# More warming products for TensorE in the run-in, and one set of weights listed two tiles later, in a kernel of dynamic convolution and maxout

## The chip, the cores and the metric

The kernel runs on one core of one Trainium2 chip. The metric is the device time of one execution in microseconds, the median of several runs. Times inside the execution are read from one profiled execution of the same kernel and count from the start of its span. PE is TensorE, DVE is VectorE, ACT is ScalarE, POOL is GpSimd and SP is SyncE, whose queue issues most DMAs.

## What is computed

Inputs are `x` (8 x 4160 x 192), `weight_gen` (8 x 4160 x 8 heads x 7 taps) and three matrices of an expert layer. Cut to what matters:

```python
w = exp(weight_gen - max) / (sum over the 7 taps + 1e-9)      # a softmax per token and head
out[b, s, h, :] = sum over k of w[b, s, h, k] * x_pad[b, s + k, h, :]   # causal, 24 elements a head
x = out.reshape(33280, 192)
h1 = x @ w1          # 192 -> 1024
h2 = x @ w2
g = maximum(h1, h2)
return g @ w_out     # 1024 -> 192
```

The kernel uses max(h1, h2) = h1 + relu(h2 - h1). It forms the difference of the two weight matrices once (`wd`) and the product `w1 @ w_out` once (`w10`), so that a result is relu(x wd) w_out + x w10.

## The kernel before

The 33280 tokens are 260 columns of 128 tokens. Columns are worked in batches of 16: batch 0 is columns 0 to 15, batch 2 columns 32 to 47. One tile is one 128x1024 block of hidden values, as much work as one column, so there are 260 tiles. They go in groups: eight of two tiles (0 to 15), then groups of three.

The work of the engines is this. ScalarE makes the weights (exponential, logarithm, exponential), applies the ReLU to the hidden values and copies results out of PSUM. VectorE multiplies `x` by the weights for all seven taps (`mul`), adds the taps (`adds`), and does the sums (`red`) and shifts (`shift`) of the softmax. TensorE does the hidden and the output products. From column 32 on, the sums are transposed by a DMA (`transpose`); for the first 32 columns TensorE sums and transposes in one step, with an identity as the moving operand:

```python
def sum_transpose(u, taps=range(K)):
    ...
    yps = ps[...].tile([P, 1024], FP32, name="yps", tag="op")
    for k in range(6):
        for t in taps:
            for r in range(2):
                nc.tensor.matmul(yps[...], lhsT=m_t[half(r), at:at + P], rhs=ident[half(r), half(r)], ...)
    yt = pyt.tile(...)
    nc.scalar.copy(out=..., in_=...)          # the cast of yps to yt
```

The softmax weights of a part of a batch are an exponential on ScalarE of what `shift` left:

```python
def shift(b, i=0, of=1):
    nc.vector.tensor_tensor(out=w_t, in0=w_t, in1=..., op=ALU.subtract)   # minus the logarithm of the sum

def weights(b, o):
    ...
    nc.scalar.activation(out=..., in_=_sub(wg_ts[b], ...), func=AF.Exp)
```

A group is listed by `hidden`. `relay` is a no-op on ScalarE that waits for the first output products, and the second ones wait for it:

```python
def hidden(g, now=(), between=lambda: None, beside=lambda: None, ahead=lambda: None):
    t0, n = GROUPS[g]
    rd = room(g)
    for t in range(t0, t0 + n - 1):
        hid_tile(t)
    if now:
        out_room(now, ...)
        last = out_first(now)
    ...
        for t in range(t0, t0 + n - 1):
            relu(rd, t, 1)
    if now:
        go = relay(last)
    hid_tile(t0 + n - 1)
    ...
    relu(rd, t0 + n - 1, 1)
    ahead()
    if now:
        out_second(now, go)
        evac(now[0] // 2, len(now) // 2)      # copies results out of PSUM, on ScalarE
    ...
```

The run-in, cut. `warm` is a PSUM tile that nothing reads:

```python
def keep_warm(times):
    for _ in range(times):
        nc.tensor.matmul(warm[:, 0:512], lhsT=ident, rhs=_sub(ident, 0, [[0, 4], [1, P]]),
                         start=True, stop=True, skip_group_check=True)

keep_warm(20)
w_diff(0, nc.scalar.copy)
sum_transpose(0)
keep_warm(2)
mul(0, 4)
nc.scalar.copy(out=w1["E"][:, HF:F], in_=ws["E", 0][:, HF:F])
hidden(0)
nc.scalar.copy(out=w1["T"], in_=ws["T", 0])
w_diff(1, nc.vector.tensor_copy)
mul(0, 8)
sum_transpose(1)
exp_sum(1)
red(1)
adds(0, 8, True)
hidden(1)
ln(1)
shift(1)
mul(0, 12)
...
def end_of_1():
    shift(2)
    adds(1, 8, True)
    mul(1, 12)
    exp_sum(3)
    red(3)
    adds(1, 12, True)

early = {
    3: (none, rest_of_1),
    4: (lambda: sum_transpose(4, LEFT), lambda: (end_of_1(), weights(2, 0))),
    5: (lambda: sum_transpose(5, LEFT), none),
    ...
}
```

In the steady stage a list says at which tile each logarithm, exponential and set of weights is put into ScalarE's queue; the logarithm of a batch (`ln`) is listed a few tiles later for later batches.

Of the kernel before, what the change touches and what calls it, by code (L numbers as in the profile page):

```python
# [17 lines left out]
def _sub(base: bass.AP, off: int, dims):  # L18
    ap = [list(base.ap[0])] + [[int(s), int(c)] for s, c in dims]
    return dataclasses.replace(base, offset=base.offset + off, ap=ap)  # L20
# [3 lines left out]
def kernel(  # L24
# [28 lines left out]
    def pieces(b):  # L53
        n = BATCHES[b][1]
        at, done = [], 0
        for w in (4, 4, 4, 4) if b < 2 else (8, 8) if n == 16 else (n,):
            at.append((done, w))
            done += w
        return at
# [81 lines left out]
    def ln(b):  # L141
        nc.scalar.activation(out=s_ts[b], in_=s_ts[b], func=AF.Ln)  # L142
# [7 lines left out]
    def weights(b, o):  # L150

        w = dict(pieces(b))[o]
        if b not in en_ts:
            en_ts[b] = pen.tile([P, 16 * WGC * 2], BF16, name="en_t", tag="en")
        J = 2 if w == 4 and b < 2 else 1
        N = w * H // J
        for j in range(J):
            nc.scalar.activation(  # L158
                out=_sub(en_ts[b], (o * WGC + j * N * K) * 2, [[2 * N, K], [2, N], [1, 2]]),
                in_=_sub(wg_ts[b], (o * H + j * N) * K, [[1, K], [K, N], [0, 2]]), func=AF.Exp,  # L160
            )
# [62 lines left out]
    def half(j):  # L224
        return slice(64 * j, 64 * j + 64)


    LEFT = (0, 1, 2, K - 1)

    def sum_transpose(u, taps=range(K)):  # L230

        b, o, n = UNITS[u]
        assert n == 4
        yps = ps["r" if "r" in ps else "o"].tile([P, 1024], FP32, name="yps", tag="op")
# [3 lines that stand above are left out]
                    at = (K * o + t * n) * D + k * P  # L238
                    nc.tensor.matmul(  # L239
                        yps[:, r * 512 + k * 64:r * 512 + (k + 1) * 64],  # L240
                        lhsT=m_t[half(r), at:at + P], rhs=ident[half(r), half(r)],
                        start=(k == 0 and t == taps[0]), stop=(t == taps[-1]),
                        skip_group_check=True,
                    )
        yt = pyt.tile([P, 8 // 2 * 3 * P], BF16, name="yt", tag="yt")
        nc.scalar.copy(out=_sub(yt, 0, [[64, 2], [P, 6], [1, 64]]),  # L246
                       in_=_sub(yps, 0, [[512, 2], [64, 6], [1, 64]]))
        yt_ts[u] = yt
# [18 lines left out]
    def hid_tile(t):  # L267


        u = TILES[t][0]  # L270
        fs, w = chunks(t)
        for f in fs:
            for s in range(3):
                for j in range(2):
                    nc.tensor.matmul(  # L275
                        hid_out(t, f, j), lhsT=wd[half(j), s * F + f * P:s * F + (f + 1) * P],
                        rhs=_sub(yt_ts[u][half(j), :], (s + j) % 3 * P, [[3 * P, w // P], [1, P]]),
                        start=(f == fs[0] and s == 0), stop=(f == fs[-1] and s == 2),
                        skip_group_check=True,
                    )  # L280

    def relu(rd, t0, n):

        (hd, at), k = hd_at[t0], rd_at[t0][1]
        nc.scalar.activation(out=rd[:, k * 1024:(k + n) * 1024], in_=hd[:, at:at + n * 1024],  # L285
                             func=AF.Relu)
# [34 lines left out]
    def out_first(now):  # L321

        for c in now[::2]:
            u, i, _ = column(c)
            for s in range(3):
                for j in range(2):
                    nc.tensor.matmul(  # L327
                        op_out(c + j),
                        lhsT=yt_ts[u][half(j), (3 * i + (s + j) % 3) * P:(3 * i + (s + j) % 3 + 1) * P],
                        rhs=w10[half(j), s * D:(s + 1) * D], start=(c == now[0] and s == 0),  # L330
                        stop=False, skip_group_check=True,
                    )
            for f in range(FCH):
                last = [out_hidden(c + j, f, j) for j in range(2)]
        return last

    def out_second(now, go):

        for c in now[::2]:
            for f in range(FCH):  # L340
                for j in range(2):
                    mm = out_hidden(c + 1 - j, f, j)
                    if c == now[0] and f == 0:
                        tc.add_manual_dep(mm.ins, go.ins.name, SYNC, reason="bank of the other half")

    def relay(last):

        go = nc.scalar.nop()  # L348
        for mm in last:
            tc.add_manual_dep(go.ins, mm.ins.name, SYNC, reason="bank of the other half")  # L350
        return go
# [50 lines left out]
    OUTS, c = [[], [], []], 0  # L402
# [8 lines left out]
    def room(g):  # L411

        t0, n = GROUPS[g]
        if "c" in ps:
            ab = ps["ab"].tile([P, 2048], FP32, name="hd2", tag="ab")
            for t in range(t0, t0 + n - 1):
                hd_at[t] = ab, (t - t0) * 1024
            hd_at[t0 + n - 1] = ps["c"].tile([P, 1024], FP32, name="hd1", tag="c"), 0
        else:
            for t in range(t0, t0 + n):  # L420
                hd_at[t] = ps["h"].tile([P, 1024], FP32, name="hdp", tag="hd"), 0
        rd = prd.tile([P, 3 * 1024], BF16, name="rd_t", tag="rd")
        for t in range(t0, t0 + n):
            rd_at[t] = (rd, t - t0)
        return rd

    def out_room(now, tag=None):
        tag = tag or ("r" if "r" in ps else "o")
        w, name = {"ab": (2048, "ab"), "c": (1024, "c")}.get(tag, (1024, "op"))
        tile_ = ps[tag].tile([P, w], FP32, name="op_ps", tag=name)  # L430
        for c in now:
            op_at[c // 2] = tile_, (c - now[0]) // 2 * D
# [9 lines that stand above are left out]
            out_room(now, "ab" if n == 1 and "ab" in ps else None)  # L442
            last = out_first(now)
        if len(now) > 2:
            relu(rd, t0, n - 1)
        else:
# [5 lines that stand above are left out]
        if len(now) > 2:  # L452
            beside()
# [4 lines that stand above are left out]
            evac(now[0] // 2, len(now) // 2)  # L458
        between()
        if len(now) <= 2:  # L460
            beside()
# [25 lines left out]
    with tc.tile_pool(name="pstage", bufs=1) as pstage:  # L487
# [101 lines left out]
        def keep_warm(times):  # L589

            for _ in range(times):
                nc.tensor.matmul(warm[:, 0:512], lhsT=ident, rhs=_sub(ident, 0, [[0, 4], [1, P]]),
                                 start=True, stop=True, skip_group_check=True)

        keep_warm(20)
        w_diff(0, nc.scalar.copy)
        sum_transpose(0)
        keep_warm(2)
        mul(0, 4)


# [67 lines left out]
# [9 lines that stand above are left out]
    none = lambda: None  # L678
    early = {
        3: (none, rest_of_1),  # L680
        4: (lambda: sum_transpose(4, LEFT), lambda: (end_of_1(), weights(2, 0))),
        5: (lambda: sum_transpose(5, LEFT), none),
        6: (lambda: (weights(2, 8), ln(3), sum_transpose(6, LEFT)), lambda: load_x(3, 0, 8)),
        7: (lambda: sum_transpose(7, LEFT), none),
    }
# [48 lines left out]
    def steps(g, tiles):  # L734

        if tiles:
            softmax_steps(g)
        for t in tiles:
            extra(t)
# [6 lines left out]
    for g in range(4, len(GROUPS)):  # L746
        if GROUPS[g][1] == 3 and "c" not in ps:
            later_ps()
        tiles = [t for t in range(GROUPS[g][0], sum(GROUPS[g])) if t >= 16]
        if g in early:  # L750
            hidden(g, OUTS[g], early[g][0], ahead=lambda: (weights(1, 12), ln(2)) if g == 4 else None)
            early[g][1]()
            steps(g, tiles)
        else:
            hidden(g, OUTS[g], beside=lambda: steps(g, tiles))
# [30 lines left out]
```

The softmax here doesn't subtract the row's maximum and nothing guards it: scores larger than these inputs give would overflow.

## Time and profile before

| | before |
|---|---|
| time, median of 3 runs | 416.42 us (416.41 to 416.79) |
| span of the profiled execution | 415.6 us |
| TensorE busy | 396.6 us, 95% |
| VectorE busy | 377.2 us, 91% |
| ScalarE busy | 359.4 us, 86% |
| GpSimd busy | 73.2 us, 18% |

A line of the time line reads: start in us, duration in us (of a run of alike instructions as one), engine, line of the kernel, operation, result <- operands, shape, count; in square brackets the idle time of that engine just before it and what ended it. A line of a stretch reads: stretch and its length, then busy time and instructions of PE, PEld (weight loads), DVE, ACT and POOL, then the granted TensorE clock, the share of the DMA engines and GB/s. A line of a DMA queue reads: packets, MB, and the time of the packets as a share.

### The profile page before, as it was taken

How to read it: one execution, taken by the hardware profiler on the slowest of the kernel's cores; microseconds unless marked ns; L12 is line 12 of the kernel's file. 1: busy time of each engine (PE TensorE's matmuls, PEld its weight loads, DVE VectorE, ACT ScalarE, POOL GpSimd, SP SyncE). 2: the span in 40 equal slices, each digit the busy share in tenths (PEclk: the TensorE clock that was granted, in tenths of full speed). 3: DMA queues.
4: the chain of work that ended last, by engine and by line, in shares of the span. 5: the costliest groups of instructions: out<-in, count | busy, mean ns of one | idle time of the engine just before them, and what ended most of it. 6: DMA issues, size and time to landing. Idle time of an engine off the chain costs nothing.

```text
span 415.6 us, 15816 instructions
## 1 busy us (share of the span) xinstructions
PE 396.6 (95%) x7262; PEld 316.6 (76%) x7262; DVE 377.2 (91%) x218; ACT 359.4 (86%) x425; POOL 73.2 (18%) x102
## 2 busy tenths in 40 slices
PE   5788899999999999999999999999999999999994
PEld 2678899777777787777877778777787777777793
DVE  5999999999999999999999999999999999998000
ACT  5798989998989998899998999989999988888761
POOL 1510101222210222221002121220122220210000
PEclk9699999999999999999999999999999999999998
DMA  8966427766656966866786498478658658635423
GB/s 235 255 170 175 108 74 166 158 166 146 171 119 124 248 154 120 232 165 103 189 203 161 93 254 184 75 241 171 131 101 245 162 103 207 150 77 191 98 79 115
DMA packets 60243, 65.68 MB, mean 158 GB/s; under 512 B 47602, under 2 KB 48498, under 8 KB 60177
## 3 DMA queue, kind: packets, MB, share of 16 engines
q1 hardware_dynamic: 51904, 40.47, 35.6%
q0 software_dynamic: 8128, 24.11, 28.3%
q8 instruction: 57, 0.93, 0.9%
q10 hardware_dynamic: 144, 0.10, 0.1%
q14 instruction: 10, 0.07, 0.1%
HBM read 35.96 MB, written 25.56 MB: 148 GB/s over the span
## 4 chain that ended last, share of the span: by engine, by line
PE 59%; DVE 21%; ACT 12%; issue 3%; DMA 3%; SPq 1%; DVEq 0%; ACTq 0%
PE op_ps L315 27%; PE hd L275 26%; DVE m_t L173 11%; ACT rd_t L285 7%; PE op_ps L327 5%; DVE m_t L189 4%; DVE m_t L195 3%; DMA ws1T<-in_moe_w_dram 2%; ACT en_t L158 1%; DMA yt<-y_t 1%; DVE wg_t L147 1%; DVE y_t L198 1%; PE hdp L275 1%; ACT o_t L371 1%; DVE sum_t L139 1%
## 5 line engine op out<-in xcount | busy, mean ns | idle before, releaser
L285 ACT ACTIVATE rd_t<-hd 128x1024 bf16<-128x1024 f32 (+1 forms) x206 | 234.6, 1188 | 28.3 <-PE hd L275 26.9
L315 PE MATMUL op_ps<-wo,rd_t 64*128 64x192 bf16 x4160 | 211.0, 243 | 1.0 <-ACTq L348 0.9
L315 PEld LDWEIGHTS <-rd_t 64*128 64x128 bf16 x4160 | 181.2, 94 | 16.8 <-ACTq L348 1.5
L275 PE MATMUL hd<-yt,wd 64*128 64x512 bf16 (+1 forms) x1584 | 187.8, 360 | 1.7 <-ACT rd_t L285 1.1
L173 DVE TENSOR_TENSOR m_t<-xb_t,en_t 128x10752 bf16<-128x10752 bf16 (+1 forms) x37 | 187.5, 5070 | 0.3 <-ACT en_t L158 0.3
L275 PEld LDWEIGHTS <-wd 64*128 64x128 bf16 x1776 | 95.4, 95 | 45.6 <-issue 5.7
L215 POOL CAST gate<-yt 128x1 f32<-128x1 bf16 x29 | 37.3, 1287 | 276.9 <-DMA yt<-y_t 276.9
L189 DVE TENSOR_TENSOR m_t<-m_t 128x4608 bf16<-128x4608 bf16 (+1 forms) x34 | 79.5, 2338 | 0.1
L371 ACT COPY o_t<-op_ps 128x384 f32<-128x384 f32 (+1 forms) x99 | 57.1, 589 | 13.4 <-PE op_ps L315 13.2
L327 PE MATMUL op_ps<-w,yt 64*128 64x192 bf16 x780 | 55.9, 243 | 1.8 <-ACT o_t L371 0.9
L327 PEld LDWEIGHTS <-yt 64*128 64x128 bf16 x780 | 38.6, 94 | 18.8 <-issue 3.5
L195 DVE TENSOR_TENSOR m_t<-m_t 128x3072 bf16<-128x3072 bf16 (+1 forms) x29 | 49.9, 1722 | 0.1
L158 ACT ACTIVATE en_t<-wg_t 128x896 bf16<-128x896 f32 (+2 forms) x45 | 35.2, 818 | 1.1 <-DVE wg_t L147 1.1
L198 DVE TENSOR_TENSOR y_t<-m_t 128x1536 bf16<-128x1536 bf16 (+1 forms) x29 | 27.3, 941 | 0.5
L361 DVE COPY o_t<-op_ps 128x192 f32<-128x192 f32 x1 | 0.4, 357 | 26.5 <-ACT o_t L361 26.5
L139 DVE TENSOR_REDUCE sum_t<-e_t 128x64 f32<-128x448 f32 (+2 forms) x30 | 19.5, 650 | 3.5 <-ACT e_t L127 3.5
L147 DVE TENSOR_TENSOR wg_t<-wg_t,sum_t 128x280 f32<-128x280 f32 (+4 forms) x45 | 22.0, 489 | 0.6 <-ACT sum_t L142 0.4
L115 POOL DMA_DIRECT2D xb_t<-in_x_dram x32 | 17.3, 539 | 24.2 <-DVE m_t L173 15.6
L127 ACT ACTIVATE e_t<-wg_t 128x896 f32<-128x896 f32 (+1 forms) x17 | 16.0, 940 | 2.8 <-DMA wg_t<-in_weight_gen_dram 2.8
L285 ACT ACTIVATE rd_t<-hdp 128x1024 bf16<-128x1024 f32 x16 | 16.1, 1033 | 1.9 <-PE hdp L275 1.9
L275 PE MATMUL hdp<-yt,wd 64*128 64x256 bf16 x192 | 14.0, 287 | 1.9 <-ACT yt L246 0.9
L239 PE MATMUL yps<-ident,m_t 64*128 64x64 bf16 x492 | 9.6, 198 | 2.9 <-DVE m_t L173 2.9
(46 smaller groups left out, 73.1 us busy)
## 6 DMA issues: line engine op xcount, KB each, us to landing
out_dram<-o_t SPq DMA_DIRECT2D x28, 768.0 KB, 4.3
xb_t<-in_x_dram POOLq DMA_DIRECT2D x28, 384.0 KB, 5.1
wg_t<-in_weight_gen_dram POOLq DMA_DIRECT2D x14, 448.0 KB, 5.9
xb_t<-xb_t POOLq DMA_DIRECT2D x16, 288.0 KB, 5.3
out_dram<-o_t SPq DMA_DIRECT2D x8, 384.0 KB, 2.7
wg_t<-in_weight_gen_dram SPq DMA_DIRECT2D x2, 448.0 KB, 4.9
xs<-in_x_dram SPq DMA_DIRECT2D x2, 384.0 KB, 6.7
xb_t<-in_x_dram POOLq DMA_DIRECT2D x1, 768.0 KB, 6.8
```

The costliest lines, as they stand in the source:

```text
L147: nc.vector.tensor_tensor(out=w_t, in0=w_t, in1=_sub(s_ts[b], hs.start, [[1, hs.stop - hs.start], [0, K]]), op=ALU.subtract)
L158: nc.scalar.activation(out=_sub(en_ts[b], (o * WGC + j * N * K) * 2, [[2 * N, K], [2, N], [1, 2]]), in_=_sub(wg_ts[b], (o * H + j * N) * K ...
L173: nc.vector.tensor_tensor(out=m_out, in0=x_in, in1=_sub(en_ts[b], o * WGC * 2, [[2, K * n * H], [0, G // 2], [1, 2]]), op=ALU.mult,)
L189: nc.vector.tensor_tensor(out=taps(0, 1, 3), in0=taps(0, 1, 3), in1=taps(3, 1, 3), op=ALU.add)
L195: nc.vector.tensor_tensor(out=taps(0, 2, 2), in0=taps(0, 2, 2), in1=taps(1, 5, 2), op=ALU.add)
L198: nc.vector.tensor_tensor(out=_sub(y_ts[b], o * D, [[64, 2], [P, 3 * w // 2], [1, 64]]), in0=taps(0, 1, 1), in1=taps(2, 1, 1), op=ALU.add,)
L215: nc.gpsimd.tensor_copy(out=gate, in_=yt[:, 0:1])
L275: nc.tensor.matmul(hid_out(t, f, j), lhsT=wd[half(j), s * F + f * P:s * F + (f + 1) * P], rhs=_sub(yt_ts[u][half(j), :], (s + j) % 3 * P, ...
L285: nc.scalar.activation(out=rd[:, k * 1024:(k + n) * 1024], in_=hd[:, at:at + n * 1024], func=AF.Relu)
L315: return nc.tensor.matmul(op_out(c), lhsT=rd[half(r), k * 1024 + at:k * 1024 + at + P], rhs=wo[half(r), f * D:(f + 1) * D], start=False, s ...
L327: nc.tensor.matmul(op_out(c + j), lhsT=yt_ts[u][half(j), (3 * i + (s + j) % 3) * P:(3 * i + (s + j) % 3 + 1) * P], rhs=w10[half(j), s * D: ...
L371: nc.scalar.copy(out=_sub(o, c % 24 * D, [[D, len(qs)], [h * D, 2], [1, D]]), in_=_sub(tile_, at + (qs[0] - p) * D, [[D, len(qs)], [512, 2 ...
```

## The change

Three edits. The warming products ahead of the first sums become 30 instead of 20, and those behind them 6 instead of 2: they are there to keep TensorE's clock up while it waits for VectorE's first product and for the first cast. And `weights(2, 0)`, the weights of columns 32 to 39, is no longer listed at the end of group 4 (tiles 8 and 9). It is listed in group 5 (tiles 10 and 11), behind the two ReLUs of that group and ahead of its copy of results, so that ScalarE comes to it later.

```diff
-        keep_warm(20)
+        keep_warm(30)
         w_diff(0, nc.scalar.copy)
         sum_transpose(0)
-        keep_warm(2)
+        keep_warm(6)
         mul(0, 4)
@@
-        4: (lambda: sum_transpose(4, LEFT), lambda: (end_of_1(), weights(2, 0))),
+        4: (lambda: sum_transpose(4, LEFT), end_of_1),
@@
-            hidden(g, OUTS[g], early[g][0], ahead=lambda: (weights(1, 12), ln(2)) if g == 4 else None)
+            hidden(g, OUTS[g], early[g][0], ahead=lambda: {4: lambda: (weights(1, 12), ln(2)), 5: lambda: weights(2, 0)}.get(g, none)())
```

## The prediction

> **What bounds the kernel now.** I read the page's totals first, then the chain that ended last, then the idle times of VectorE, TensorE and ScalarE, because three engines are nearly full and a total cannot say which of them sets the end.
>
> ```profile
> PE 396.6 (95%) x7262; PEld 316.6 (76%) x7262; DVE 377.2 (91%) x218; ACT 359.4 (86%) x425; POOL 73.2 (18%) x102
> PE 59%; DVE 21%; ACT 12%; issue 3%; DMA 3%; SPq 1%; DVEq 0%; ACTq 0%
> ```
>
> VectorE's 91% is an average: table 2 of the page has it at 9 tenths until slice 36 and then almost nothing. Until 345 us it is practically never idle. The chain in order of time lies on TensorE from 52 to 260 us, on VectorE from 261 to 344 us, then passes through one transposing DMA to TensorE. The crossing in the time line:
>
> ```profile
> 344.12 5.75 DVE L173 TENSOR_TENSOR m_t<-xb_t,en_t 128x10752 bf16<-128x10752 bf16 x1
> 344.35 1.27 SPq L207 DMA_TRANSPOSE yt<-y_t  x1
> 349.56 0.82 PE L275 MATMUL hd<-yt,wd 64*128 64x512 bf16 x6 [0.60 <-DMA yt<-y_t]
> ```
>
> The transposing DMA is issued 0.15 us after VectorE's last add, and TensorE stands still 0.60 us until it lands. It is TensorE's only wait of any size after 300 us; afterwards TensorE works through to the end. So the end is the later of two runners at this point: VectorE plus one DMA, and TensorE, which is only 0.60 us behind in need. A gain has to reach **both** to reach the end.
>
> The early stage shows where either can gain. The granted clock of one stretch, TensorE's early groups, and VectorE's first wait in the run-in:
>
> ```profile
> 13.35:20.20 6.85, 5.91 (x122) 4.56 (x116) 6.71 (x7) 5.51 (x7) 2.59 (x5) 0.50 1.25 223
> ```
> ```profile
> 12.12 1.43 PE L239 MATMUL yps<-ident,m_t 64*128 64x64 bf16 x84 [2.90 <-DVE m_t L173]
> 13.48 1.03 PE L592 MATMUL warm<-ident 128*128 128x512 bf16 x2
> 15.46 2.74 PE L275 MATMUL hdp<-yt,wd 64*128 64x256 bf16 x24 [0.94 <-ACT yt L246]
> 17.97 2.41 PE L239 MATMUL yps<-ident,m_t 64*128 64x64 bf16 x84
> ```
> ```profile
> 20.42 0.80 ACT L246 CAST yt<-yps 128x768 bf16<-128x768 f32 x1 [0.23 <-PE yps L239]
> 21.11 0.95 ACT L127 ACTIVATE e_t<-wg_t 128x896 f32<-128x896 f32 x1
> 22.10 1.09 DVE L139 TENSOR_REDUCE sum_t<-e_t 128x128 f32<-128x896 f32 x1 [0.72 <-ACT e_t L127]
> ```
>
> The clock is half for 6.85 us: PEclk, the third number from the end, is 0.50. The same 84 small products take 1.43 us at full clock and 2.41 at half; ScalarE's cast waits for them, its exponential stands behind the cast, and VectorE waits 0.72 us for that exponential. The second place:
>
> ```profile
> 40.50 1.09 DVE L147 TENSOR_TENSOR wg_t<-wg_t,sum_t 128x896 f32<-128x896 f32 x1
> 41.62 1.04 ACT L158 ACTIVATE en_t<-wg_t 128x896 bf16<-128x896 f32 x1 [1.05 <-DVE wg_t L147]
> 41.70 0.61 PEld L315 LDWEIGHTS <-rd_t 64*128 64x128 bf16 x16 [1.17 <-ACTq L348]
> ```
>
> ScalarE stands 1.05 us at the weights of columns 32 to 39 because VectorE has just begun their shift, and TensorE stands behind ScalarE's no-op.
>
> **What the Trainium skill says.** "TensorE: Matmul & The Clock Gate", Part 1 (The HAM clock gate): the array runs at half clock until a free-running window of about 3.4 us has been busy, and returns to half after an idle one. The trace agrees: the warming products start 0.43 us apart, 0.21 us after 6.40 us; the clock falls at about 13.36 us and returns at about 20.19, 6.83 us or two windows. Counted back on that grid, the window from 9.95 to 13.36 held 1.2 us of work and lost the clock. The window from 6.54 to 9.95 held some 2.6 us and kept it. "PSUM — Partial Sum Buffer", Engine vs sequencer instructions: ScalarE's queue is strictly first in, first out, and a no-op runs on its sequencer. The trace agrees: the no-op passes 0.08 us after the blocked exponential starts, before the ReLU listed ahead of it begins at 42.56. "DMA: Bandwidth & Descriptors", Queues, rings and completion order: each DMA engine takes its queues in turn, a packet at a time. I use it below for why one transpose is slow; the trace shows the coincidence, not the cause.
>
> **Part 1, the warming products.** Ten more at 0.21 us take 2.1 us: they end at 9.22 + 2.1 = 11.3 us, inside the 2.90 us in which TensorE waited for VectorE's product, so they delay nothing. The window to 13.36 then holds about 1.4 + 1.2 = 2.6 us of work and should keep the clock. Six products behind the first sums then take 6 x 0.21 = 1.3 us and end near 14.8, ahead of 15.46, when the cast ends for which the hidden products wait. Those 24 take 1.48 us (as the same group does later at full clock) and not 2.74; the next 84 start at 16.9 (VectorE's product is done at 16.13) and end near 18.4 instead of 20.4. On ScalarE: ReLU from 16.3 to 18.25 (two, 1.0 each), the cast of w1 to 19.2, the cast of the sums to 19.9, the exponential from 19.8 to 20.75. Before, it started at 21.11, so ScalarE gains 1.3 us. VectorE is free at 18.42 + 2.96 = 21.4; its 0.72 us wait vanishes. What follows on VectorE needs ScalarE results that are also 1.3 us earlier, so I count **0.72 us for VectorE, 1.3 us for ScalarE and TensorE**. Nothing is taken away: 14 products and 14 loads are added, all into idle time.
>
> **Part 2, the weights two tiles on.** The 1.04 us activation is moved, not removed. Its old place made ScalarE wait for VectorE's shift, which ends at 41.6 - 0.7 = 40.9 after part 1. ScalarE would be there at 40.56 - 1.3 = 39.3. In the new place two ReLUs come first (39.3 to 41.2), so the shift is done, the weights end near 42.1, and the copy of results starts near 42.0 instead of 44.37: TensorE and ScalarE are now **2.3 us** ahead (1.3 from part 1, about 1.0 from the wait). VectorE needs these weights only at 47.90 - 0.7 = 47.2, so it gains and loses nothing here.
>
> **Two small waits further on.** VectorE's long product starts 5.67 us ahead of its successor everywhere but at two places, 166.24 to 172.11 and 237.44 to 243.29 (0.20 and 0.18 us more). There ScalarE's logarithm ended only just before (171.74 + 0.34). ScalarE, 2.3 us ahead and VectorE 0.7, leaves no such wait: VectorE's gain becomes 0.72 + 0.38 = **1.1 us**.
>
> **The sum at the crossing.** TensorE's next unit starts at the later of its own arrival (348.96 - 2.3 = 346.7) and the landing (349.5 - 1.1 = 348.4). With the DMA as it was, the end moves 1.1 us. But that DMA took 5.2 us against a median of 3.8. The fetch of instructions explains it better than any store. DMA queues from 347.0 to 347.5 us:
>
> ```profile
> q1 hardware_dynamic: 248, 0.06, 443.0%
> q8 instruction: 1, 0.02, 11.6%
> ```
>
> One 16 KB fetch of instructions falls into the transpose, and a trickle of a few GB/s follows. Of the eight transposes issued from 178 to 345 us that took 4.2 us or more, seven have such a fetch begin 0 to 3 us after their issue (read in steps of 0.75 us; the one issued near 202.6 us has none); the quick ones have it outside that stretch or at its edges. The fetch follows TensorE's stream, which is moved against VectorE by 1 us or more, and lies about 0.8 us earlier again since 28 instructions precede it (estimate: a fetch of 256 instructions each 7.2 us in this stretch). I expect it 1 us after the issue, where the earlier cases took 4.3 to 4.9 us (0.3 to 0.9 us off), perhaps clear of it (1.4 us off). TensorE's units before that one had 1.0 us or more in hand, so being gated there first caps the gain at about VectorE's 1.1 plus 1.8.
> So the gain is 1.1 + (0 to 1.4), and I choose 1.5: 416.4 - 1.5 = **414.9 us**.
>
> **Rivals.** (a) *The clock falls all the same*, since the small products fill half the array. Six warming products at 0.43 us end at 16.05 and delay the hidden products 0.6 us: part 1 loses 0.6 at ScalarE, VectorE waits 1.3; with part 2's recovered lead and the two small waits, 416.2 to 416.8. For it: 2.4 us of work from 13.36 to 16.77 did not win the clock back. Against it: between 40.66 and 44.07 about 2.3 us of busy time did not lose it. One in seven. (b) *Only TensorE gains*: VectorE finds another releaser behind its 0.72 us (the logarithm, or a load), and TensorE waits longer at the crossing. VectorE's next steps show no wait, so this is weak: 416.0 to 416.4. (c) *The transpose misses the fetch*, so TensorE's gain goes through more fully: 414.0 to 414.3. (d) *A later unit becomes the gate*: the one issued at 366.62 had 2.2 us in hand, with its fetch 3 us after issue; a collision there leaves 1.1 + 0.7 us, 414.6.
>
> **Range and chances.** Main line 414.5 to 415.3, (c) below it, (a) and (b) above: 413.9 to 416.2 holds it 8 times in 10. 2% is 8.3 us. The whole waiting in reach is under 3 us, so either side has one chance in a hundred.
>
> **What would show it.** Right: full clock from 13 to 20 us; the second 84 sums in about 1.4 us; no VectorE wait at its second reduction; no ScalarE wait at the moved weights and none of TensorE behind the no-op; 5.67 us at both small places; the unit at the crossing issued near 343.2 and TensorE waiting there longer than 0.60 us. Wrong: a clock of 0.50 anywhere after 7 us, VectorE's transposes issued no earlier than before, or a new TensorE wait after 350 us.

## The result, and the profile after

The changed kernel takes **413.95 us** (median of 6 runs, 413.64 to 414.42). The kernel before took 416.25 us on the same chip (6 runs, 414.86 to 416.79). The ratio is 0.9953, with a 95% interval of 0.9935 to 0.997. The gain is 2.3 us, against 1.5 predicted. Six executions are few for this kernel, as the experiments show: 148 others of the kernel before have a median of 415.66 us, from which the gain would be 1.7 us.

In the two profiles the span falls by more, from 415.6 to 412.1 us, because the profiled execution of the kernel before was one of its longer ones (417.39 us against a median of 416.25). So the 3.5 us of the profiles say where time went, and the 2.3 us of the runs say how much.

The page's totals and the shares of the chain that ended last:

```profile
PE 397.0 (96%) x7276; PEld 316.0 (77%) x7276; DVE 376.9 (91%) x218; ACT 359.2 (87%) x425; POOL 76.8 (19%) x102
PE 44%; DVE 36%; ACT 12%; issue 3%; DMA 3%; SPq 1%; DVEq 0%; ACTq 0%
```

Fourteen products more on TensorE, and nothing else has changed in amount. A part of the chain has moved from TensorE (59% before, 44% now) to VectorE (21% before, 36% now).

The run-in. First one stretch (busy time and count of PE, PEld, DVE, ACT and POOL, then the granted clock, DMA share, GB/s), then TensorE's groups and the lines of ScalarE and VectorE from the time line:

```profile
13.35:20.20 6.85, 6.16 (x153) 4.74 (x152) 6.71 (x7) 6.40 (x9) 2.89 (x6) 1.00 1.24 220
```
```profile
5.55 6.05 PE L592 MATMUL warm<-ident 128*128 128x512 bf16 x24
11.83 1.40 PE L239 MATMUL yps<-ident,m_t 64*128 64x64 bf16 x84 [0.23 <-DVE m_t L173]
13.16 1.47 PE L592 MATMUL warm<-ident 128*128 128x512 bf16 x6
15.32 1.49 PE L275 MATMUL hdp<-yt,wd 64*128 64x256 bf16 x24 [0.69 <-ACT yt L246]
16.62 1.40 PE L239 MATMUL yps<-ident,m_t 64*128 64x64 bf16 x84
```
```profile
19.64 0.96 ACT L127 ACTIVATE e_t<-wg_t 128x896 f32<-128x896 f32 x1
21.00 1.08 DVE L139 TENSOR_REDUCE sum_t<-e_t 128x128 f32<-128x896 f32 x1
```

The clock is 1.00 where it was 0.50. The wait of 2.90 us before the first sums is filled up to 0.23 us. The second 84 sums take 1.40 us instead of 2.41, ScalarE's exponential starts at 19.64 instead of 21.11, and VectorE's second reduction follows its own stream, without the wait of 0.72 us. It starts 1.10 us earlier; 0.30 of this was there already at VectorE's first product (9.11 before, 8.81 now), which the change doesn't touch.

The place of the moved weights, from the time line:

```profile
39.82 1.03 ACT L285 ACTIVATE rd_t<-hdp 128x1024 bf16<-128x1024 f32 x1
40.73 1.04 ACT L158 ACTIVATE en_t<-wg_t 128x896 bf16<-128x896 f32 x1
41.64 0.49 ACT L371 COPY o_t<-op_ps 128x384 f32<-128x384 f32 x1
42.18 0.42 PE L327 MATMUL op_ps<-w,yt 64*128 64x192 bf16 x6 [0.81 <-ACT o_t L371]
```

ScalarE no longer waits for the shift. It copies results out at 41.64 instead of 44.37, 2.7 us earlier. The weights now stand ahead of that copy, though, and TensorE waits 0.81 us for it. Before, it waited there three times: 0.89 us for the no-op, 0.39 for a ReLU and 0.45 for this copy:

```profile
44.91 0.42 PE L327 MATMUL op_ps<-w,yt 64*128 64x192 bf16 x6 [0.45 <-ACT o_t L371]
```

The crossing, from the time line, with TensorE's last wait before it:

```profile
323.57 1.47 PE L275 MATMUL hd<-yt,wd 64*128 64x512 bf16 x12 [0.81 <-ACT rd_t L285]
...
342.60 5.75 DVE L173 TENSOR_TENSOR m_t<-xb_t,en_t 128x10752 bf16<-128x10752 bf16 x1
342.83 2.44 SPq L207 DMA_TRANSPOSE yt<-y_t  x1
345.91 1.78 PE L275 MATMUL hd<-yt,wd 64*128 64x512 bf16 x12
346.87 0.33 PEld L275 LDWEIGHTS <-wd 64*128 64x128 bf16 x5 [0.43 <-issue]
```

VectorE's product starts at 342.60 instead of 344.12. The transpose lands 4.12 us after its issue, at 346.95, where it took 5.29 (both read from the first use that waits for it). TensorE stands about 0.3 us inside the group of 12 products (1.78 us, where such a group takes 1.47) and not 0.60. It had already been held once, at 323.57: the record names a ReLU, but the transpose issued at 319.17 landed at 323.55, 0.02 us before.

So the 3.5 us between the profiles are: VectorE at the crossing 1.52, the transpose's landing 5.29 - 4.12 = 1.17, and what follows it 0.8. These 0.8 us all lie behind TensorE's last product, most of them in the last store: the instruction that waits for it ends 5.3 us after its issue before and 4.4 after.

### The profile page after: what moved, and what is told of

Same layout as the page of the kernel before. It is cut to its first block, busy times and chain, and to the rows that moved or that the text cites. A ratio compares the mean times of both kernels' runs of the same rounds, so it can differ in the third digit from the quotient of the medians.

```text
span 412.1 us, 15844 instructions
## 1 busy us (share of the span) xinstructions
PE 397.0 (96%) x7276; PEld 316.0 (77%) x7276; DVE 376.9 (91%) x218; ACT 359.2 (87%) x425; POOL 76.8 (19%) x102
## 4 chain that ended last, share of the span: by engine, by line
PE 44%; DVE 36%; ACT 12%; issue 3%; DMA 3%; SPq 1%; DVEq 0%; ACTq 0%
PE op_ps L315 21%; PE hd L275 19%; DVE m_t L173 18%; DVE m_t L189 8%; ACT rd_t L285 7%; DVE m_t L195 5%; PE op_ps L327 4%; DMA xs<-in_x_dram 2%; DVE y_t L198 2%; DVE sum_t L139 2%; DVE wg_t L147 1%; ACT en_t L158 1%; DMA yt<-y_t 1%; ACT yt L246 1%; PE hdp L275 1%
## 5 line engine op out<-in xcount | busy, mean ns | idle before, releaser
L275 PEld LDWEIGHTS <-wd 64*128 64x128 bf16 x1776 | 94.0, 94 | 45.8 <-issue 4.9
L215 POOL CAST gate<-yt 128x1 f32<-128x1 bf16 x29 | 41.4, 1429 | 273.3 <-DMA yt<-y_t 273.3
L275 PE MATMUL hdp<-yt,wd 64*128 64x256 bf16 x192 | 13.0, 269 | 1.9 <-ACT rd_t L285 1.1
L592 PE MATMUL warm<-ident 128*128 128x512 bf16 x36 | 10.1, 445 | 3.0 <-DVE ident L530 3.0
```

Source lines behind the costliest of these rows:

```text
L215: nc.gpsimd.tensor_copy(out=gate, in_=yt[:, 0:1])
L275: nc.tensor.matmul(hid_out(t, f, j), lhsT=wd[half(j), s * F + f * P:s * F + (f + 1) * P], rhs=_sub(yt_ts[u][half(j), :], (s + j) % 3 * P, ...
```

## The experiments

Every kernel is compared with the kernel before, run on the same chip. Two things beside the time are read for each. One is the **mean granted clock of every execution**, because the half clock of the run-in turned out not to come each time. If the clock is half for two windows of 3.4 us, the mean is 1 - 0.5 x 6.83 / 415 = 0.992; for one window it is 0.996. Up to 2.9 us of half clock at the end of the span, when TensorE has nothing left to do, come on top in the profiles: the one of the kernel before has 9.7 us of it in all and a mean of 0.988. The other is the crossing: when VectorE's product starts there, when an instruction fetch begins relative to the issue of the transpose (in steps of 0.5 us, so at -1.5 it is over before the issue), and how long the transpose takes to land.

Of 148 executions of the kernel before on three chips, 37 had a mean clock under 0.9925 (median 416.14 us), 20 lay between that and 0.9965 (416.24), and 91 had at least 0.9965 (415.16). So one execution in four loses the clock in the run-in for two windows, which goes with about 1.0 us, and at most 4 in 10 lose it at all; some of the 20 may owe their mean to the end of the span. "Full clock" below means the last group. It is far from uniform (414.15 to 417.31 us), but its medians on the three chips agree within 0.2 us. Three executions of over 590 us, one each of the kernel before, of its repeat and of the kernel with one more VectorE sum, are left out.

### The two parts alone

**Part 1 alone**, with the weights in their old place:

```diff
-        keep_warm(20)
+        keep_warm(30)
...
-        keep_warm(2)
+        keep_warm(6)
```

> Part 1 alone (30 and 6 warming products, the weights of columns 32 to 39 in their old place). Theory (the run-in clock frees VectorE, VectorE sets the crossing): full clock from 13 to 20 us, VectorE's wait of 0.72 us at its second reduction gone, the two small waits of 0.2 us near 172 and 243 us still there because ScalarE is blocked at the weights until VectorE's shift and so leads VectorE by no more than before; crossing 0.7 to 0.8 us earlier, end 0.7 us earlier, up to 1.3 more or less as the transposing DMA there is slow or not. Rival (the move of the weights makes the gain): end unchanged within 0.3 us.

Measured: 416.21 us (22 runs), ratio 1.0013 (1.0003 to 1.0024): **no gain, slightly slower**. The clock was kept (20 of 22 executions at full clock, none under 0.9925), and yet those 20 took 416.21 us. The time line of TensorE and then of ScalarE and VectorE:

```profile
50.75 0.81 PE L275 MATMUL hd<-yt,wd 64*128 64x256 bf16 x11 [0.19 <-ACT rd_t L285]
52.42 0.94 PE L275 MATMUL hd<-yt,wd 64*128 64x256 bf16 x13 [0.86 <-issue]
```
```profile
171.48 0.33 ACT L142 ACTIVATE sum_t<-sum_t 128x128 f32<-128x128 f32 x1
171.84 0.45 DVE L147 TENSOR_TENSOR wg_t<-wg_t,sum_t 128x280 f32<-128x280 f32 x1 [0.86 <-ACT sum_t L142]
```

In the midst of a unit of 24 products TensorE stands 0.86 us for nothing that the profile shows. ScalarE follows TensorE, so its logarithm at 171.48 is late, and VectorE, which had gained in the run-in, waits 0.86 us for it and gives its gain back. The transpose at the crossing took 4.85 us (fetch at +1.5).

**Part 2 alone** (the change with 20 and 2 warming products):

```diff
-        4: (lambda: sum_transpose(4, LEFT), lambda: (end_of_1(), weights(2, 0))),
+        4: (lambda: sum_transpose(4, LEFT), end_of_1),
...
-            hidden(g, OUTS[g], early[g][0], ahead=lambda: (weights(1, 12), ln(2)) if g == 4 else None)
+            hidden(g, OUTS[g], early[g][0], ahead=lambda: {4: lambda: (weights(1, 12), ln(2)), 5: lambda: weights(2, 0)}.get(g, none)())
```

> Part 2 alone (20 and 2 warming products, the weights two tiles on). Theory: half clock from 13.4 to 20.2 us and the 0.72 us wait stay; TensorE and ScalarE 1.0 us ahead after 42 us; the two small waits near 172 and 243 us go, so VectorE is 0.4 us earlier at the crossing and the end 0.4 us earlier. Rival (the move makes the gain): end 2 us earlier.

Measured: 414.33 us (22 runs), ratio 0.9978 (0.9965 to 0.9992). At full clock 414.11 (10 executions), with the half clock 415.9 (6). The profiled execution lost the clock, with 1.30 us of PEld and 2.32 of PE busy in the first window:

```profile
13.35:16.75 3.40, 2.32 (x24) 1.30 (x18) 3.37 (x3) 2.46 (x4) 1.19 (x2) 0.53 1.09 237
```

So at full clock the kernel with the moved weights is 415.16 - 414.11, about 1.0 us, faster, though VectorE doesn't wait for them in either place.

**One half of the warming at a time**, with the weights moved: 30 and 2 products, then 20 and 6.

```diff
-        keep_warm(6)        # first kernel: 30 and 2
+        keep_warm(2)
...
-        keep_warm(30)       # second kernel: 20 and 6
+        keep_warm(20)
```

> The changed kernel with 30 products ahead but only 2 behind the first sums. Theory (a window of 3.4 us must be busy enough): the clock stays full to 16.8 us; from 13.4 to 16.8 about 1.8 us of work is left, which is between the 1.2 us that lost the clock and the 2.3 us that kept it, so the clock may go at 16.8 us; if it stays the run is like the changed kernel and the four products are not needed; if it goes, the second sums take 2 us and VectorE's wait is 0 to 0.5 us. Rival (all 14 are needed): clock lost at 13.4 us and the end as with part 2 alone.

> The changed kernel with 20 products ahead and 6 behind. Theory: clock lost at 13.4 us, the six products take 0.43 us each and end near 16.0 us, which delays the first hidden products 0.6 us; that window is then nearly full and the clock comes back at 16.8 us instead of 20.2; second sums end near 19.4 us, VectorE's wait shrinks from 0.72 to under 0.2 us. End 0.2 to 0.5 us later than the changed kernel. Rival: as part 2 alone.

Measured: 415.23 us with the ten ahead alone (14 runs, ratio 0.999, 0.9977 to 1.0003) and 414.77 with the four behind alone (14 runs, ratio 0.9982, 0.9965 to 0.9998). The ten ahead leave no execution under 0.9925 and five of 14 between that and 0.9965. The four behind leave one of 14 under 0.9925 and four between. Their profiles have full clock and the moved weights, and the kernels are still 1.3 and 0.8 us slower than the change as a whole. The waits of TensorE late in the first, then in the second (us in total, times, longest):

```profile
PE hd L275 <- DMA yt<-y_t: 1.9, 2, 1.7
```
```profile
PE hd L275 <- DMA yt<-y_t: 2.1, 2, 1.8
```

The longest wait is one unit ahead of the crossing, at 324.98 and 324.71 us: the transpose there took 5.36 and 5.50 us, with a fetch at +3.0, where the change's took 4.38. At the crossing the fetches fell 2.5 and 3.0 us after the issue, and the transposes took 5.19 and 5.35 us. The two kernels differ from the whole change by 8 and 20 instructions of TensorE.

### Is it the clock, the lead, or the stream of instructions?

**The kernel before once more**, unchanged, to see how far one program differs from itself.

> The kernel before once more, for a second profile. In two thirds of its executions the mean granted clock is 0.997 or more, in the profile of record it was 0.988. Theory A (the half clock of the run-in comes and goes with the phase of the window): a profile with clock 0.997 shows full clock from 13 to 20 us without the ten and four products, no 0.72 us wait of VectorE at its second reduction, and instead a wait of about 0.9 us at the shift near 172 us, behind ScalarE's logarithm. Rival: the half clock from 13.4 to 20.2 us is there in every execution.

Measured: 415.65 us (17 runs), ratio 0.9998 (0.9983 to 1.0012). Its profile caught an execution with full clock, without any change. One stretch of it, then the waits of TensorE:

```profile
13.35:16.75 3.40, 1.99 (x38) 1.59 (x38) 3.37 (x3) 2.95 (x5) 1.09 (x2) 1.00 1.10 238
```
```profile
PE yps L239 <- DVE m_t L173: 1.5, 1, 1.5
PE hd L275 <- DMA yt<-y_t: 0.6, 1, 0.6
```

VectorE's second reduction is at 21.14 there and does not wait. Nor is there the wait of about 0.9 us near 172 us that I expected. Its product at the crossing starts at 342.89, 0.29 us behind the changed kernel's 342.60. The span is 412.8 us, and the transpose still lands only after 5.35 us (fetch at +2.5). TensorE's last product ends at 408.25 us, in the changed kernel at 406.72. **So between two profiles with full clock the 1.53 us that the change gains up to there are 0.29 of VectorE and 1.23 of the landing.**

**28 more instructions without the warming**: 14 small products (64x64) behind the 20.

```diff
         keep_warm(20)
+        for _ in range(14): nc.tensor.matmul(warm[0:64, 0:64], lhsT=ident[:, 0:64], rhs=ident[:, 0:64], ...)
```

> The kernel before, with 14 small products (64x64, into the tile that nothing reads) behind the first 20 warming products: 28 TensorE instructions more, as part 1 has, but with 0.4 us of work in idle time. Theory F (28 more instructions move the fetches of instructions, which makes TensorE stand 0.86 us near 52 us in the run of part 1 alone): the same stall here, and a median near 416.2 us as part 1 alone has. Rival (part 1 itself costs): no such stall, median as the kernel before, 415.7 us.

Measured: 416.27 us (14 runs), ratio 1.0019 (1.0004 to 1.0034), at full clock 416.06. That is part 1 alone, without its warming. The same stall and the same wait are in the time line:

```profile
52.09 0.93 PE L275 MATMUL hd<-yt,wd 64*128 64x256 bf16 x13 [0.67 <-issue]
...
171.52 0.45 DVE L147 TENSOR_TENSOR wg_t<-wg_t,sum_t 128x280 f32<-128x280 f32 x1 [0.69 <-ACT sum_t L142]
```

It is thus not the warming that costs part 1 its gain, but that 28 instructions precede nearly all the others.

**Part 1 with another count of instructions**: 24 large and 54 small products for the 30, 96 instructions more than part 1 alone.

```diff
-        keep_warm(30)
+        keep_warm(24)
+        for _ in range(54): nc.tensor.matmul(warm[0:64, 0:64], lhsT=ident[:, 0:64], rhs=ident[:, 0:64], ...)
```

> Part 1 alone with 96 more instructions (24 large and 54 small products ahead instead of 30 large). Theory F: the stall near 52 us moves or goes, and the time falls by 0.5 to 1 us from the 416.2 us of part 1 alone, to about 415.3, the time of the kernel before in its executions with full clock. Rival (part 1 itself costs): 416.2 us stays.

Measured: 414.0 us (13 runs, all at full clock), ratio 0.9958 (0.9943 to 0.9973): 2.2 us less than part 1 alone and as fast as the whole change, with the weights in their old place. The unit that stalled runs through:

```profile
51.11 1.49 PE L275 MATMUL hd<-yt,wd 64*128 64x256 bf16 x24 [0.19 <-ACT rd_t L285]
```

The fetch at the crossing is at -1.5, and the transpose lands in 3.79 us.

**Two logarithms listed two tiles earlier** in the kernel before, and nothing else. This is the second place where the lead of TensorE and ScalarE could reach VectorE.

```diff
-            ln_at = -2 if c == 4 else 0 if c < 8 else 2 if c < 11 else 4
+            ln_at = -2 if c == 4 else 0 if c < 9 else 2 if c < 12 else 4
```

> The kernel before with two logarithms (of batches 8 and 11) listed two tiles earlier, where the list goes over to later places. Theory L (VectorE's gain in the run-in is given back at these two logarithms, which follow TensorE): VectorE's waits near 172 and 243 us go, VectorE is 0.4 us (half clock) to 1.1 us (full clock) earlier at the crossing, and the end 0.4 to 0.7 us earlier than the kernel before on the same chip, limited then by TensorE's own arrival. Rival (the two waits are incidental): no change beyond 0.2 us.

Measured: 414.89 us (22 runs), ratio 0.998 (0.9968 to 0.9993); at full clock 414.51 (13) against 415.16. The logarithm now runs at 164.00 and VectorE goes through 171 us without a wait. But the repeat of the kernel before, also at full clock, has no wait there either, and VectorE's product at the crossing starts only 0.03 us earlier than in it (342.86). What differs is the transpose, with 4.15 us instead of 5.35; TensorE's last product ends 0.45 us earlier (407.80). So it isn't shown that the wait for the logarithm is part of what the change removes at full clock; in the half-clock profile it was 0.20 us.

### The stream alone, and both together

**124 more instructions in the kernel before**, 70 small and 12 large products for its 20 large ones; they end when the 20 did, so nothing is warmed.

```diff
-        keep_warm(20)
+        for _ in range(70): nc.tensor.matmul(warm[0:64, 0:64], lhsT=ident[:, 0:64], rhs=ident[:, 0:64], ...)
+        keep_warm(12)
```

> The kernel before, with 70 small warming products (64x64) and 12 large ones ahead of the first sums in place of 20 large ones: 124 more TensorE instructions, ending when the 20 did, so with no warming added and the weights in their old place. Theory (the stream of instruction fetches is what moved the time of the other variants): at 256 instructions a fetch and 7.2 us a fetch, 124 instructions bring each fetch about 3.5 us earlier; the one at +2.5 us of the crossing transpose falls near -1.0, the transpose lands in 3.8 to 4.0 us, and executions that keep full clock take 414.0 to 414.5 us against 415.2 of the kernel before, executions with half clock about 0.8 more. Rival (the lead of TensorE or of VectorE is what counts): 415.2 to 415.7, as before, whatever the landing.

Measured: 414.19 us (7 runs), ratio 0.9958 (0.994 to 0.9976). **That is nearly the whole gain of the change, with neither of its parts.** The clock is lost as before, in 3 of 7 executions (414.66 us) and not in 4 (413.82), and the groups are 1.5 and 1.3 us faster than the same groups of the kernel before (2.0 and 1.2 against those on the same chip). The profile caught the half clock:

```profile
13.35:20.20 6.85, 5.92 (x115) 4.64 (x116) 6.71 (x7) 5.30 (x7) 3.02 (x6) 0.52 1.23 221
```
```profile
343.54 5.75 DVE L173 TENSOR_TENSOR m_t<-xb_t,en_t 128x10752 bf16<-128x10752 bf16 x1
343.77 1.27 SPq L207 DMA_TRANSPOSE yt<-y_t  x1
...
347.56 1.48 PE L275 MATMUL hd<-yt,wd 64*128 64x512 bf16 x12
```

VectorE is at the crossing only 0.58 us earlier than in the half-clock profile of the kernel before. The transpose, with the fetch at -1.5, lands in 3.79 us instead of 5.29.

**The changed kernel with 56 more instructions**, 26 large and 32 small products for the 30.

```diff
-        keep_warm(30)
+        keep_warm(26)
+        for _ in range(32): nc.tensor.matmul(warm[0:64, 0:64], lhsT=ident[:, 0:64], rhs=ident[:, 0:64], ...)
```

> The changed kernel with 26 large and 32 small warming products ahead of the first sums in place of 30 large: 56 more TensorE instructions and the same length. Theory: the fetch at +0.5 us of the crossing transpose comes 1.6 us earlier, to -1.1, and is clear of it; the landing falls from 4.1 to 3.8 us; 413.5 to 413.9 us against 413.95. Rival: the fetches of other stages move into other transposes and give back the 0.3 us: 414.0 to 415.0, with a TensorE stall or a wait behind a transpose elsewhere.

Measured: **413.25 us** (5 runs, 412.89 to 413.58), ratio 0.9935 (0.9915 to 0.9954). It is the fastest kernel of this study; it ran at another time than the changed kernel (413.64 to 414.42), but the two ranges don't meet. The DMA queues from 342 to 349 us, in 40 slices, of this kernel and then of the kernel before in its full-clock profile:

```profile
GB/s 0 0 0 0 0 0 0 0 0 0 0 9 170 222 215 200 212 211 221 212 190 218 539 261 527 492 421 246 492 527 421 316 421 492 351 386 456 492 316 351
q1 hardware_dynamic: 1793, 1.68, 74.3%
```
```profile
GB/s 0 0 0 0 0 0 0 0 0 0 0 0 0 123 228 222 203 202 208 218 215 195 274 395 234 0 0 1 7 9 10 9 149 140 421 562 562 386 176 562
q1 hardware_dynamic: 1664, 0.98, 75.0%
q8 instruction: 1, 0.02, 0.8%
```

In the first, the transpose moves some 210 GB/s until it is done, and stores follow at once. In the second a fetch (q8) falls into the stretch, and behind the transpose's 210 GB/s there is a gap of about 1.2 us at 0 to 10 GB/s before its last bytes and the stores.

### Which runner sets the end?

**One more VectorE sum** in the changed kernel, near tile 104, into a tile that nothing reads:

```diff
         s = o + k
+        if t == 104: nc.vector.reduce_sum(out=scr, in_=..., axis=AX.X)
```

> The changed kernel with one more VectorE sum (128x128 out of 128x896) listed near tile 104, into a tile that nothing reads, about 0.5 to 1.1 us. Theory (VectorE and one DMA are what TensorE waits for at the crossing, and TensorE has little in hand): the end moves by 0.4 to 1.1 us, 414.4 to 415.0. Rival (TensorE alone sets the end): 413.7 to 414.1, and the wait of TensorE at the crossing grows from next to nothing to less than the added time.

**Six more TensorE products** in the changed kernel, those of tile 100 done twice:

```diff
-        for f in fs:
+        for f in (fs + fs if t == 100 else fs):
```

> The changed kernel with the hidden products of tile 100 done twice, the same result, 6 more products of 512 columns, about 1.3 us of TensorE. Theory (both runners bind, TensorE by what it has in hand at the crossing, some 0.2 to 0.5 us): the end moves by 0.8 to 1.3 us, 414.8 to 415.3. Rival (VectorE and the transpose alone set it): 413.7 to 414.2, and TensorE's wait at the crossing shrinks.

Measured: 415.00 us with VectorE's sum (20 runs, ratio 0.9982, 0.997 to 0.9994) and 414.05 with TensorE's products (9 runs, ratio 0.9954, 0.9937 to 0.9972), against 413.95 of the changed kernel. VectorE's sum and the product that follows it:

```profile
176.92 1.08 DVE L718 TENSOR_REDUCE scr<-wd 128x128 f32<-128x896 bf16 x1
177.91 5.75 DVE L173 TENSOR_TENSOR m_t<-xb_t,en_t 128x10752 bf16<-128x10752 bf16 x1
```

0.99 us of VectorE arrive whole: its product at the crossing is 0.96 us later (343.56), the transpose takes nearly the same (4.21 us), and the time is 1.0 us longer. TensorE's six products take 0.65 us from start to start, and not the 1.3 us that I wrote down. They are not seen in the time. TensorE's next wait in the time line shows where they went:

```profile
323.52 1.47 PE L275 MATMUL hd<-yt,wd 64*128 64x512 bf16 x12 [0.41 <-DMA yt<-y_t]
```

The wait at 323.5 us is 0.41 us instead of 0.81, and the stand at the crossing 0.14 instead of 0.31 (the group of 12 takes 1.61 us). In the changed kernel VectorE and its transposing DMAs set the end, and TensorE has over half a microsecond in hand.

### All of them together

| kernel | TensorE instructions added | weights moved | us at full clock (executions) | VectorE's product at the crossing | fetch | landing, us | product + landing |
|---|---|---|---|---|---|---|---|
| before (profile: the repeat) | 0 | no | 415.16 (91) | 342.89 | +2.5 | 5.35 | 348.24 |
| logarithms earlier | 0 | no | 414.51 (13) | 342.86 | +3.0 | 4.15 | 347.01 |
| part 2 alone (profile: half clock) | 0 | yes | 414.11 (10) | 343.71 | +0.5 | 4.29 | 348.00 |
| four behind | 8 | yes | 414.74 (9) | 342.64 | +3.0 | 5.35 | 347.99 |
| ten ahead | 20 | yes | 415.24 (9) | 343.05 | +2.5 | 5.19 | 348.24 |
| small products | 28 | no | 416.06 (8) | 343.56 | +2.5 | 5.15 | 348.71 |
| part 1 alone | 28 | no | 416.21 (20) | 343.85 | +1.5 | 4.85 | 348.70 |
| **the change** | 28 | yes | 413.92 (5) | 342.60 | +0.5 | 4.12 | 346.72 |
| the change, 56 more | 84 | yes | 413.25 (5) | 342.68 | -1.5 | 3.80 | 346.48 |
| part 1, 96 more | 124 | no | 414.00 (13) | 343.12 | -1.5 | 3.79 | 346.91 |
| 124 more (profile: half clock) | 124 | no | 413.82 (4) | 343.54 | -1.5 | 3.79 | 347.33 |

Neither the warming nor the weights order the times. The sum of VectorE's start and the landing does, roughly. In seven of these profiles TensorE's last product ends 60.0 to 60.1 us after it. With the logarithms earlier and in the last three rows it is 60.4 to 61.0 us: there something later than this landing sets the end. Behind TensorE's last product come another 4.5 to 6.4 us, mostly the last store (4.56 in the repeat, 5.39 in the change, 6.36 with the four behind, whose profiled execution took 416.14 us and not the 414.74 of the table). That differs by as much as the change gains, so a single span can't rank these kernels. The counts of instructions do not order it in a simple way, since each change also moves TensorE against VectorE.

## Why the prediction was right or wrong

The total was inside the range, 0.95 us under the 414.9 predicted and close to the lower edge. The steps fared differently, and part of the agreement is luck: at full clock most of the gain is a transpose that happened to land sooner, and with 8 or 20 added instructions in place of 28 it did not.

**Right, as written.** The filled wait keeps the clock, and the numbers of part 1's chain came close: hidden products 15.32 (predicted at 15.46 or later), second sums 16.62 (16.9), exponential 19.64 (19.8), reduction without a wait. Rival (a), the clock falling all the same, did not come: in 72 executions with the ten large products added ahead, in five kernels, the mean clock was never under 0.9925. (The stretch from 40.66 to 44.07, which I cited against it, held 2.13 us of work and not 2.3.) The copy at 41.64 (42.0) and the 2.3 us of lead for ScalarE (2.7 measured at that copy, of which TensorE loses 0.81 at 42.18) came too. So did the end of the two small waits: the logarithm runs at 168.68 instead of 171.74 (at full clock, the first of them isn't there in the kernel before either). VectorE's gain was to be 1.1 us and is 1.52 at the crossing, of which 0.30 are the earlier start of its first product. The cap by TensorE being gated one unit earlier was named, and it is there at 323.57. The wait that I wanted to see grow past 0.60 us at the crossing shrank to 0.3 for that reason.

**The step that failed is "0.72 us for VectorE" as a constant gain of part 1.** It was read from one profile, and I took its half clock for a property of the kernel. It is a property of one execution in four, and of 4 in 10 at most. The Trainium skill has this in "TensorE: Matmul & The Clock Gate", Part 1: the activity window is free-running and doesn't begin with the kernel, so the same kernel varies from run to run. I cited the window and counted it back from one execution as if it stood still. The runs agree with the page: the wait ahead of the first sums lost the clock in 37 to 57 of 148 executions. In the profile of the kernel before, most of the wait falls into one window (9.95 to 13.36), which is left with 1.24 us of work; in the repeat the windows lie 1.0 us earlier, two of them share the wait (1.87 and 2.01 us of work), and the clock stays. Worth about 1.0 us where it is lost, the clock is some 0.25 to 0.4 us of the gain on the average (1.0 us times these shares, an estimate), not 0.72 and what hung on it. At full clock the change still gains 415.16 - 413.92 = 1.2 us.

**The second failed step is that "nothing is taken away" by 28 added instructions.** Alone they cost 0.9 us at full clock (416.06 against 415.16), by a stall of TensorE near 52 us that reached VectorE through the logarithm at 172 us. Part 1 alone gained nothing for that reason. I had named the shift of the fetches, but only for the crossing. In the whole change, where the moved weights let TensorE pass that unit at 49.06 instead of 51.78 us, the stall doesn't appear: with this count of instructions the two parts need each other, and their gains can't be added (-0.2% for part 2 and +0.1% for part 1 alone, -0.5% for both).

**Mis-sized: the landing.** I expected the fetch 1 us after the issue and a landing 0.3 to 0.9 us sooner; it was at +0.5 and 1.17 us sooner. This term, which I added last, is the largest single one after VectorE's own against the half-clock profile, and at full clock it is 1.23 of 1.53 us. That the fetch matters, and isn't just a coincidence, rests on the kernel with 124 instructions more: nothing but the stream and the sizes of the warming products is changed, and it gains 1.3 us at full clock. It cannot be said that all 1.3 us are the crossing's, since every other stage's fetches moved as well.

**Rivals.** (b), that only TensorE gains, is refuted in its form, but part 1 alone shows its mechanism: VectorE did find the logarithm behind its 0.72 us. (c), the transpose that misses the fetch, came halfway in the change and fully in the version with 56 instructions more (413.25, below the 414.0 that I gave it). (d) wasn't seen.

**Left open.** Why TensorE stands 0.7 to 0.9 us near 52 us is shown in part. The traces place the stall at a seam of the instruction stream. Counting TensorE's products and weight loads in order of time, it comes ahead of number 1987 in both kernels that show it. All 15 waits of over 0.09 us that the 14 profiles put down to "issue" for TensorE after 9 us come ahead of number 449, 1218, 1219 or 1987, which are 768 to 770 apart, three times the 255 or so that one fetch serves, and each ends 2.2 to 2.6 us after the latest fetch began. One of them, in the repeat of the kernel before, has its fetch at 34.29 us:

```profile
36.80 0.61 PE L239 MATMUL yps<-ident,m_t 64*128 64x64 bf16 x29 [0.60 <-issue]
```

So TensorE has most likely run to the end of what had been fetched; no run delays a fetch to test that. That two fetches follow each other closely is not enough: both kernels with the stall have two 3.5 us apart around it, but so has the kernel before (51.09 and 54.63), and waits 0.17 us there. Nor is it known why a fetch makes the rest of a transpose trickle. Where a fetch will fall could be told for two large additions (-1.0 and -1.1 expected, -1.4 and -1.2 in the traces), but with 8 and 20 instructions it fell where it hurts, against what the kernel with 28 would have suggested.

## What to carry to other kernels

Where two engines are balanced to within a microsecond, as here, a change of 0.5% can come from where the instruction stream lies and not from what the change is for. Test it with a version that adds idle instructions and leaves the change out, and one that keeps the change and adds some; here the first took most of the credit and the second gave the best kernel. And before a wait in a profile is counted as a gain, look at several executions: the half clock that misled me here is there in at most four of ten.

## What the runs showed of the hardware

**A fetch of instructions and a transposing DMA.** The page counts the fetches:

```profile
q8 instruction: 57, 0.93, 0.9%
```

57 fetches of 16 KB for 2 x 7276 instructions of TensorE are one for 255 instructions, every 7.2 us. Over 294 transposes issued after 150 us in the profiles of this study, the landing by the step in which a fetch began after the issue was, as a median: 4.03 us at 0 (23 cases), 4.35 at 0.5 (19), 4.46 at 1.0 (13), 4.58 at 1.5 (17), 5.18 at 2.0 (10), 5.29 at 2.5 (7), 4.12 at 3.0 (50, from 3.77 to 5.56), and 3.80 with none in that stretch (155).

**How little work keeps the clock.** The traces record when the clock changes, and so the places of the windows of 3.41 us. In the three profiles that lost the clock, the window ahead of the loss held 1.23, 1.24 and 1.48 us of PE. In the other eleven the emptiest window held 1.70 us (the ten ahead alone, from 322.76), and in the run-in 1.87. Once the clock was half, a window with 2.33 to 2.48 us did not bring it back, and a full one did. The window that lost it in the kernel before, and the one in the repeat that kept it:

```profile
9.95:13.36 3.41, 1.24 (x84) 1.24 (x84) 3.41 (x4) 2.87 (x8) 2.49 (x4) 1.00 1.05 318
```
```profile
8.95:12.36 3.41, 1.87 (x35) 0.89 (x35) 3.41 (x2) 3.06 (x8) 1.52 (x2) 1.00 1.03 315
```
